# A fused attention and expert kernel: four buffers for the raw words of the dense weights, and their loads issued ahead

## Chip, core and metric

One Trainium2 chip, one core. The metric is the device time of one execution in microseconds (us); of several runs the median is given.

## What is computed

Three parts follow one another. Random-feature attention (4 batches, 8 heads, 576 positions, 64 wide, 128 features) makes `x` of 2304 rows by 512. A dense layer with a hidden width of 2048 follows, and then a layer of eight experts, of which each row takes one.

```python
q_p, k_p = phi(q_s), phi(k_s)              # exp(proj - sq - max), 128 features
num = q_p @ (k_p.T @ v); den = q_p @ k_p.sum() + 1e-6
x = num / den                              # 2304 x 512, heads side by side
h = x @ w_in                               # 512 x 2048, words of 64 bits
x = np.maximum(0.01 * h, h) @ w_out        # 2048 x 512, words of 64 bits
e = argmax(x @ w_gate)                     # one of 8 experts per row
out = gate * eom * (np.maximum(x @ w1[e], 0) @ w2[e])
```

`w_in` and `w_out` come in as float64, and so do not go into TensorE as they lie in memory: each has to be made into float32 on the core, and each float32 into a high part (`float32r`) and a low part. A product is three matmuls: high by high, high by low, low by high.

## The kernel before

**Tiles and loops.** The rows are cut into nine chunks of 256 (`c`), the hidden width into eight units of 256 (`u`). For each pair `(c, u)` `h_unit` makes the hidden values in PSUM (`hp`, 24 matmuls, L494 to L496) and evacuates them (`g`, L499 on ScalarE, then `gh` and `gl`), and `x_unit` multiplies by `w_out` into the accumulators (`acc`, 12 matmuls, L514 to L516). The pairs of the chunks 0 and 1 are woven (sorted by 2u, and 2u + 5 for chunk 1); then chunk follows chunk. In between, `tick` runs one stage of each attention item in flight: its loads (`xpair`, `nat`, `vb` on SyncE), squares (L284 on ScalarE), projection (`pw`, L313), exponentials (`h`, L342), transposes (`qtp`, `xtp`) and evacuations (`et`, `xh`, `xl`). `hp`, `qtp`, `xtp` and `nump` share two PSUM buffers at that time.

**The dense weights.** A unit has two half tiles of `w_in` and two of `w_out`; `order` lists the 32 half tiles, here called k = 0 to 31, unit by unit, `in` before `out`. `load_w` treats one:

- SyncE loads 512 KB of 64-bit words into `wraw` (L188 or L200). The tag has two buffers. `issue_after(newest[-1])` keeps the load behind the newest load of attention.
- ScalarE scales the upper words into `w` (L205; tag `w32`, two buffers).
- VectorE masks and shifts (L206), adds the sign (L207) and the lower word's bits (L208).
- ScalarE casts to the high part `wih` or `woh` (L210), GpSimd subtracts in two pieces to the low part `wil` or `wol` (L212).

The converted tiles lie in the ring `wring`, 32 places of 4 KB per partition; later the experts' weights go round in it. Before the pairs begin, k = 0 to 7 are treated. Then, in each step of chunk 0, `load_w` is called until 4(u + 2) half tiles are done, so the weights of unit u + 1 are treated in step u, just before the `h_unit` that reads them is written for the first of them.

**What sets the order.** The code is written in this sequence, and a scheduler orders each engine's instructions by when it expects them to be ready. Every engine then runs its queue in order and waits at the instruction whose inputs or buffer are missing. SyncE's queue holds all loads but the gathers.

Of the kernel before, what the change touches and what calls it, by code (L numbers as in the profile page):

```python
# [14 lines left out]
I32 = mybir.dt.int32  # L15
# [6 lines left out]
P = 128  # L22
# [21 lines left out]
WPRE = 8  # L44
WFROM = 0
WU = 6
TAIL = 9
# [40 lines left out]
def tile_kernel(ctx: ExitStack, tc: tile.TileContext, kT, k_nat, v_nat, qT, q_nat, om, w_in, w_out, wg, w1, w2, out, stop=None, dbg=None):  # L88
    nc = tc.nc
# [3 lines left out]
    wring = ctx.enter_context(tc.tile_pool(name="wring", bufs=32))  # L93
# [39 lines left out]
    wst = ctx.enter_context(tc.tile_pool(name="wst", bufs=2))  # L133

    with ExitStack() as pa:
# [41 lines left out]

        def load_w(kind, u, half, pool):

            raw = pool.tile([P, 512, 2], I32, name="wraw", tag="wraw")  # L180
            if kind == "in":
# [4 lines left out]
                wh, wl = win[u]  # L186
                with tc.issue_after(newest[-1]):
                    nc.sync.dma_start(raw.rearrange("p (i a) b -> p i (a b)", i=2),  # L188
                                      w_in[2 * half * P:2 * (half + 1) * P, u * 256:(u + 1) * 256].bitcast(I32).rearrange("(i p) a -> p i a", i=2))
                wh, wl = wh[:, 2 * half:2 * half + 2, :], wl[:, 2 * half:2 * half + 2, :]  # L190
                wh, wl = wh.rearrange("p a b -> p (a b)"), wl.rearrange("p a b -> p (a b)")
            else:
# [4 lines left out]
                wh, wl = wout[u]  # L197
                f = 2 * u + half
                with tc.issue_after(newest[-1]):
                    nc.sync.dma_start(raw.rearrange("p a b -> p (a b)"), w_out[f * P:(f + 1) * P, :].bitcast(I32))  # L200
                wh, wl = wh[:, half, :], wl[:, half, :]
            top, low = raw[:, :, 1], raw[:, :, 0]
            w = pool.tile([P, 512], I32, name="w32", tag="w32")

# [17 lines left out]
        order = [(k, u, h) for u in range(NU) for k in ("in", "out") for h in range(2)]  # L222
        loaded = 0
# [482 lines left out]
        for i in range(first + LEAD):  # L706
            tick(seq.pop(0) if i < first + NEW else None)
            while loaded < min(WPRE, (i - WFROM) * WPRE // (first + LEAD - WFROM)):
                load_w(*order[loaded], wst)
                loaded += 1  # L710
# [207 lines left out]
        for i, (c, u) in enumerate(pairs):  # L918
# [9 lines left out]
            while c == 0 and loaded < min(len(order), max(4 * (u + 2), WPRE + int(u * (32 - WPRE) / WU))):  # L928
                load_w(*order[loaded], wst)
                loaded += 1  # L930
            if i + 1 < len(pairs):
                gg[pairs[i + 1]] = h_unit(*pairs[i + 1])
# [191 lines left out]
```

## Time and profile before

| what | us |
|---|---|
| median of 3 runs (821.76 to 823.11) | 822.12 |
| the profiled execution | 822.98 |
| its span, first to last instruction | 821.3 |
| TensorE's matmuls busy in the span | 802.7 |
| VectorE busy | 440.0 |
| ScalarE busy | 370.0 |
| GpSimd busy | 161.0 |

The span is what lies between the first and the last instruction on the core; 1.7 us of the execution lie around it. The busy times are sums over stages that have different limits, so for this change the stretch from 46 us (the first `hp`) to 160 us (the last converted weight) is to be read by itself. Granted clock of TensorE: 1.00 of full speed (2.4 GHz) in each 20 us from the start to 200 us.

### The profile page before, as it was taken

What the parts mean: (1) busy time and instruction counts of PE and PEld (TensorE: products, weight loads), DVE (VectorE), ACT (ScalarE), POOL (GpSimd) and SP (SyncE); (2) the same over time, 40 slices, a digit from 0 to 9 for tenths busy, and PEclk for the clock granted to TensorE, in tenths of its full rate; (3) what the DMA queues carried; (4) which work ended last, traced back from release to release, by engine and by line L of the source; (5) the groups of instructions that cost most, each with busy time, mean ns of one, the idle gap of its engine ahead of it and who ended that gap; (6) DMA issues with size and microseconds to landing.
All of it is one profiled execution on the core that took longest, in us unless ns stands there. A gap on an engine that the chain in (4) does not pass through costs nothing. (4 is left out here: it accounts for less than half of the span.)

```text
span 821.3 us, 15800 instructions
## 1 busy us (share of the span) xinstructions
PE 802.7 (98%) x6061; PEld 712.0 (87%) x6061; DVE 440.0 (54%) x1118; ACT 370.0 (45%) x1239; POOL 161.0 (20%) x204
## 2 busy tenths in 40 slices
PE   9999999999999999999999999999999999999996
PEld 6777777888898988898899898888889989999995
DVE  6987799736645654544554543545644444343220
ACT  4886778625545656426435233122323343332210
POOL 3524444301211211011010000021014231130101
PEclk9999999999999999999999999999999999999998
DMA  6735665403312342022011000037316654150101
GB/s 211 229 124 178 176 194 181 141 1 91 66 47 61 94 67 59 26 44 70 28 33 21 27 1 1 27 114 99 78 34 205 171 166 140 58 163 24 46 14 34
DMA packets 45153, 72.74 MB, mean 89 GB/s; under 512 B 5905, under 2 KB 27665, under 8 KB 45074
## 3 DMA queue, kind: packets, MB, share of 16 engines
q1 hardware_dynamic: 41554, 62.22, 27.6%
q0 software_dynamic: 3520, 9.47, 3.8%
q8 instruction: 49, 0.80, 0.5%
q14 instruction: 30, 0.25, 0.1%
HBM read 61.08 MB, written 10.59 MB: 87 GB/s over the span
## 5 line engine op out<-in xcount | busy, mean ns | idle before, releaser
L494 PE MATMUL hp<-xh,wih 128*128 128x256 f32 x576 | 163.6, 284 | 0.8 <-ACT g L499 0.4
L496 PE MATMUL hp<-xh,wil 128*128 128x256 f32 x576 | 161.4, 280 | 2.0 <-POOL wil L212 2.0
L495 PE MATMUL hp<-xl,wih 128*128 128x256 f32 x576 | 161.1, 280 | 0.6 <-DVE xl L219 0.6
L514 PE MATMUL acc<-woh,gh 128*128 128x512 f32 x288 | 117.1, 406 | 1.2 <-ACT h L342 1.2
L516 PE MATMUL acc<-woh,gl 128*128 128x512 f32 x288 | 114.6, 398 | 0.1
L515 PE MATMUL acc<-wol,gh 128*128 128x512 f32 x288 | 114.7, 398 | 0.0
L494 PEld LDWEIGHTS hp<-xh,wih 128*128 128x128 f32 x576 | 108.1, 188 | 3.8 <-ACT g L499 0.5
L496 PEld LDWEIGHTS hp<-xh,wil 128*128 128x128 f32 x576 | 108.1, 188 | 3.5 <-POOL wil L212 3.2
L495 PEld LDWEIGHTS hp<-xl,wih 128*128 128x128 f32 x576 | 108.1, 188 | 2.7 <-DVE xl L219 1.0
L342 ACT ACTIVATE h<-pw,bias 128x128 f32<-128x128 f32 x288 | 84.2, 370 | 33.1 <-DVE bias L334 25.9
L501 DVE SCALAR_TENSOR_TENSOR g<-hp,g 128x512 f32<-128x512 f32 x56 | 38.6, 689 | 97.0 <-ACT g L499 96.6
L499 ACT COPY g<-hp 128x512 f32<-128x512 f32 x72 | 42.2, 587 | 100.6 <-PE hp L496 96.7
L795 PE MATMUL eht<-exh,ewh 128*128 128x256 f32 (+1 forms) x256 | 76.6, 299 | 0.0
L797 PE MATMUL eht<-exh,ewl 128*128 128x256 f32 (+1 forms) x256 | 75.5, 295 | 0.0
L796 PE MATMUL eht<-exl,ewh 128*128 128x256 f32 (+1 forms) x256 | 75.5, 295 | 0.0
L219 POOL TENSOR_TENSOR rawl<-xpair,rawh 128x256 fp32r<-128x256 f32 x38 | 29.0, 763 | 204.6 <-ACT rawh L216 198.8
L284 ACT ACTIVATE nat<-nat 128x64 f32<-128x64 f32 x224 | 55.4, 257 | 27.8 <-DVE bias L334 19.3
L798 ACT ACTIVATE ehh<-eht 128x256 fp32r<-128x256 f32 (+1 forms) x64 | 26.4, 412 | 91.3 <-PE eht L797 89.9
L516 PEld LDWEIGHTS acc<-woh,gl 128*128 128x128 f32 x288 | 54.1, 188 | 13.0 <-DVE gl L219 1.0
L514 PEld LDWEIGHTS acc<-woh,gh 128*128 128x128 f32 x288 | 54.1, 188 | 11.7 <-ACT h L342 1.4
L515 PEld LDWEIGHTS acc<-wol,gh 128*128 128x128 f32 x288 | 54.1, 188 | 9.2
L799 DVE SCALAR_TENSOR_TENSOR ehl<-eht,ehh 128x256 fp32r<-128x256 f32 (+1 forms) x64 | 29.2, 456 | 52.8 <-ACT ehh L798 49.2
(176 smaller groups left out, 1668.3 us busy)
## 6 DMA issues: line engine op xcount, KB each, us to landing
eraw<-w SPq DMA_DIRECT2D x32, 512.0 KB
wraw<-w_in SPq DMA_DIRECT2D x16, 512.0 KB
wraw<-w_out SPq DMA_DIRECT2D x16, 512.0 KB
x_d<-rows SPq DMA_DIRECT2D x9, 514.0 KB
xpair<-qT SPq DMA_DIRECT2D x18, 256.0 KB
nat<-k_nat SPq DMA_DIRECT2D x27, 128.0 KB
xpair<-kT SPq DMA_DIRECT2D x12, 256.0 KB
nat<-q_nat SPq DMA_DIRECT2D x23, 128.0 KB
```

The costliest lines, as they stand in the source:

```text
L284: nc.scalar.activation(nat[:, j], nat[:, j], AF.Square, scale=math.sqrt(sc * sc / 2.0), accum_out=s2[:, j:j + 1])
L342: st["e_last"] = nc.scalar.activation(h[:, j, :], src[:, j // 2, j % 2], AF.Exp, bias=bias[:, j:j + 1], scale=sc).ins
L494: nc.tensor.matmul(hp[:, i, :], a, xh[:, d, :], start=d == 0, stop=False)
L495: nc.tensor.matmul(hp[:, i, :], a, xl[:, d, :], start=False, stop=False)
L496: nc.tensor.matmul(hp[:, i, :], b_, xh[:, d, :], start=False, stop=d == ND - 1)
L499: last_g[:] = [nc.scalar.copy(g, hp).ins]
L514: nc.tensor.matmul(acc[t], a, h_, start=u == 0 and i == 0, stop=False)
L515: nc.tensor.matmul(acc[t], a, l_, start=False, stop=False)
L516: nc.tensor.matmul(acc[t], b_, h_, start=False, stop=u == NU - 1 and i == 1)
L795: nc.tensor.matmul(t, wh, self.xh[:, d, 0:n], start=d == 0, stop=False)
L796: nc.tensor.matmul(t, wh, self.xl[:, d, 0:n], start=False, stop=False)
L797: nc.tensor.matmul(t, wl, self.xh[:, d, 0:n], start=False, stop=d == ND - 1)
```

## The change

Two tiles `spare` are taken from the ring `wring` ahead of all others, as 64-bit raw buffers. The load is cut out of `load_w` into `fetch_w(k)`. For k = 8 to 27 the two halves of `w_out` (k % 4 is 2 or 3) go into the spare tiles, the halves of `w_in` into the two `wraw` buffers as before; k below 8 and from 28 on use `wraw` alone. After the conversions of a step of chunk 0 the loads of the next four half tiles are issued, so that they are in the queue one step earlier. The conversion itself, its `w` buffers and the amount of data are as they were. The ring has 32 places for 34 requests now: the last two (`w_out` of unit 7) take the places of the spare tiles.

```diff
--- before.py
+++ after.py
@@ -43,6 +43,7 @@
 LAG = 2
 WPRE = 8
 WFROM = 0
+SPARE = 2
 WU = 6
 TAIL = 9
 KQ = 8
@@ -175,18 +176,37 @@
         win = [None] * NU
         wout = [None] * NU
 
-        def load_w(kind, u, half, pool):
-
-            raw = pool.tile([P, 512, 2], I32, name="wraw", tag="wraw")
+        spare = [wring.tile([P, 512, 2], I32, name="wspare", tag="w") for _ in range(SPARE)]
+        raws = {}
+
+        def fetch_w(k):
+
+            kind, u, half = order[k]
+            if WPRE <= k < 28 and k % 4 >= 2:
+                raw = spare[k % 4 - 2]
+            else:
+                raw = wst.tile([P, 512, 2], I32, name="wraw", tag="wraw")
+            raws[k] = raw
+            with tc.issue_after(newest[-1]):
+                if kind == "in":
+                    nc.sync.dma_start(raw.rearrange("p (i a) b -> p i (a b)", i=2),
+                                      w_in[2 * half * P:2 * (half + 1) * P, u * 256:(u + 1) * 256].bitcast(I32).rearrange("(i p) a -> p i a", i=2))
+                else:
+                    f = 2 * u + half
+                    nc.sync.dma_start(raw.rearrange("p a b -> p (a b)"), w_out[f * P:(f + 1) * P, :].bitcast(I32))
+
+        def load_w(k):
+
+            if k not in raws:
+                fetch_w(k)
+            raw = raws[k]
+            kind, u, half = order[k]
             if kind == "in":
                 if win[u] is None:
                     wh = wring.tile([P, ND, 2 * P], F32R, name="wih", tag="w")
                     wl = wring.tile([P, ND, 2 * P], F32R, name="wil", tag="w")
                     win[u] = (wh, wl)
                 wh, wl = win[u]
-                with tc.issue_after(newest[-1]):
-                    nc.sync.dma_start(raw.rearrange("p (i a) b -> p i (a b)", i=2),
-                                      w_in[2 * half * P:2 * (half + 1) * P, u * 256:(u + 1) * 256].bitcast(I32).rearrange("(i p) a -> p i a", i=2))
                 wh, wl = wh[:, 2 * half:2 * half + 2, :], wl[:, 2 * half:2 * half + 2, :]
                 wh, wl = wh.rearrange("p a b -> p (a b)"), wl.rearrange("p a b -> p (a b)")
             else:
@@ -195,12 +215,9 @@
                     wl = wring.tile([P, 2, D], F32R, name="wol", tag="w")
                     wout[u] = (wh, wl)
                 wh, wl = wout[u]
-                f = 2 * u + half
-                with tc.issue_after(newest[-1]):
-                    nc.sync.dma_start(raw.rearrange("p a b -> p (a b)"), w_out[f * P:(f + 1) * P, :].bitcast(I32))
                 wh, wl = wh[:, half, :], wl[:, half, :]
             top, low = raw[:, :, 1], raw[:, :, 0]
-            w = pool.tile([P, 512], I32, name="w32", tag="w32")
+            w = wst.tile([P, 512], I32, name="w32", tag="w32")
 
             nc.scalar.activation(w.bitcast(F32), top.bitcast(F32), AF.Copy, scale=2.0 ** -112)
             nc.vector.tensor_scalar(w, w, 0x0FFFFFFF, 3, op0=ALU.bitwise_and, op1=ALU.logical_shift_left)
@@ -706,7 +723,7 @@
         for i in range(first + LEAD):
             tick(seq.pop(0) if i < first + NEW else None)
             while loaded < min(WPRE, (i - WFROM) * WPRE // (first + LEAD - WFROM)):
-                load_w(*order[loaded], wst)
+                load_w(loaded)
                 loaded += 1
 
 
@@ -926,8 +943,12 @@
                 at = [(ps_x, "x"), (ps_x, "x")] if c != 1 else [(ps_proj, "pj"), (ps_a, "a")]
                 acc[c] = [ps.tile([P, D], F32, name=f"acc{t}", tag=tag) for t, (ps, tag) in enumerate(at)]
             while c == 0 and loaded < min(len(order), max(4 * (u + 2), WPRE + int(u * (32 - WPRE) / WU))):
-                load_w(*order[loaded], wst)
+                load_w(loaded)
                 loaded += 1
+            if c == 0:
+                for k in range(loaded, min(len(order), loaded + 2 + SPARE)):
+                    if k not in raws:
+                        fetch_w(k)
             if i + 1 < len(pairs):
                 gg[pairs[i + 1]] = h_unit(*pairs[i + 1])
             if c == NCH - 1 and u == 0:
```

The lines shift: what was L188 is L192, L200 is L196, L205 is L222, L210 is L227, L216 is L233, L253 is L270, L267 is L284, L342 is L359, L401 is L418, L433 is L450 and L499 is L516.

SyncE's queue from the load of k = 7 (the first row) on; `wraw` and `wspare` are raw words, `xpair`, `nat` and `vb` attention's. Before:

```order
L200 DMA wraw<-w_out 128x1024
L253 DMA xpair<-kT 128x2x256 x2
L267 DMA nat<-k_nat 128x256 x2
L188 DMA wraw<-w_in 128x2x512 x2
L267 DMA nat<-k_nat 128x256
L200 DMA wraw<-w_out 128x1024
```

And changed:

```order
L196 DMA wraw<-w_out 128x1024
L270 DMA xpair<-kT 128x2x256
L192 DMA wraw<-w_in 128x2x512
L196 DMA wspare<-w_out 128x1024 x2
L192 DMA wraw<-w_in 128x2x512
L284 DMA nat<-k_nat 128x256
L270 DMA xpair<-kT 128x2x256
L284 DMA nat<-k_nat 128x256
L192 DMA wraw<-w_in 128x2x512
```

The loads of k = 8, 10, 11 and 9 stand ahead of one `xpair` and the first `nat`; before, k = 8 and 9 stood behind these and behind a second `nat`.

ScalarE's queue about the copy `g` of the eighth hidden unit in order of pairs (`g_1713`); `w32_1648`, `w32_1658`, `w32_1670` and `w32_1680` are the words of k = 20 to 23 in the kernel before:

```order
L210 CAST wih_1645<-w32_1648 128x512
L205 ACTIVATE w32_1658<-wraw_1656 128x512
L499 COPY g_1713<-hp_1688 128x512
L401 COPY kv1_1258<-kvp_1544 128x132
L216 CAST gh_1716<-g_1713 128x512
L205 ACTIVATE w32_1670<-wraw_1666 128x512
L210 CAST wih_1645<-w32_1658 128x512
L433 COPY et_1768<-qtp_1763 128x512
L210 CAST woh_1667<-w32_1670 128x512
L205 ACTIVATE w32_1680<-wraw_1678 128x512
```

Changed, at the same `g`; `w32_1674` is k = 23, and `w32_1917`, `w32_1925`, `w32_1935` and `w32_1943` are k = 24 to 27:

```order
L222 ACTIVATE w32_1917<-wraw_1682 128x512
L227 CAST woh_1664<-w32_1674 128x512
L222 ACTIVATE w32_1925<-wraw_1684 128x512
L516 COPY g_1713<-hp_1688 128x512
L227 CAST wih_1915<-w32_1917 128x512
L418 COPY kv1_1262<-kvp_1546 128x132
L233 CAST gh_1716<-g_1713 128x512
L222 ACTIVATE w32_1935<-wspare_141 128x512
L227 CAST wih_1915<-w32_1925 128x512
L222 ACTIVATE w32_1943<-wspare_142 128x512
L450 COPY et_1768<-qtp_1763 128x512
```

At the same place the queue is four half tiles further on, and L222 (L205 before) of k = 25 and 27 stands directly behind the cast of k = 23 and 25, whose word lay in the buffer that it writes.

## Rows read from the trace of the kernel before

**Rows 1.** Table by stretches: us, busy us (count) of PE, PEld, DVE, ACT, POOL.

```profile
70.00:122.00 52.00, 49.31 (x389) 40.44 (x389) 43.36 (x81) 36.77 (x128) 19.54 (x23) 1.00 0.59 180
122.00:160.00 38.00, 36.41 (x276) 29.12 (x275) 34.89 (x79) 29.57 (x109) 17.62 (x22) 1.00 0.55 175
46.00:160.00 114.00, 107.26 (x844) 87.44 (x845) 96.99 (x206) 87.20 (x323) 46.14 (x54) 1.00 0.56 172
...
200.00:300.00 100.00, 100.00 (x862) 89.33 (x858) 55.02 (x162) 52.94 (x235) 17.37 (x21) 1.00 0.30 65
```

**Rows 2.** Waits of TensorE, 46 to 160 us: total us, times, longest.

```profile
PE hp L496 <- POOL wil L212: 2.0, 5, 0.6
PE acc L514 <- ACT h L342: 1.2, 1, 1.2
PE pw L313 <- ACT h L342: 1.0, 2, 0.7
PE hp L495 <- DVE xl L219: 0.6, 1, 0.6
PE qtp L431 <- ACT g L499: 0.5, 1, 0.5
PE qtp L431 <- DVE xr L451: 0.5, 1, 0.5
PE hp L494 <- ACT g L499: 0.4, 1, 0.4
```

**Rows 3.** Waits of TensorE's weight loads, 46 to 160 us.

```profile
PEld hp L496 <- POOL wil L212: 3.2, 6, 0.8
```

**Rows 4.** Timeline of SyncE: start us, us, line, transfer.

```profile
53.86 0.34 SPq L267 DMA_DIRECT2D nat<-k_nat  x1
54.30 0.89 SPq L188 DMA_DIRECT2D wraw<-w_in  x2
...
74.44 0.38 SPq L188 DMA_DIRECT2D wraw<-w_in  x1
```

**Rows 5.** Timeline of ScalarE about half tile k = 13; idle time before in brackets.

```profile
78.33 0.67 ACT L205 ACTIVATE w<-wraw 128x512 f32<-128x512 f32 x1 [2.70 <-DMA wraw<-w_in]
...
79.89 1.13 ACT L342 ACTIVATE h<-pw,bias 128x128 f32<-128x128 f32 x4
...
82.54 0.62 ACT L210 CAST wih<-w 128x512 fp32r<-128x512 f32 x1 [0.53 <-DVE w L208]
83.06 0.66 ACT L205 ACTIVATE w<-wraw 128x512 f32<-128x512 f32 x1
```

**Rows 6.** Timeline of GpSimd: the subtractions of k = 9, 11 and 13.

```profile
65.90 2.33 POOL L212 TENSOR_TENSOR wil<-w,wih 128x256 fp32r<-128x256 f32 x2 [2.30 <-ACT wih L210]
...
74.45 1.44 POOL L212 TENSOR_TENSOR wol<-w,woh 128x256 fp32r<-128x256 f32 x2 [4.63 <-ACT woh L210]
...
83.24 1.61 POOL L212 TENSOR_TENSOR wil<-w,wih 128x256 fp32r<-128x256 f32 x2 [1.28 <-ACT wih L210]
```

**Rows 7.** Timeline of TensorE at the first of the waits for k = 13.

```profile
84.02 0.38 PE L496 MATMUL hp<-xh,wil 128*128 128x256 f32 x1 [0.31 <-POOL wil L212]
```

**Rows 8.** Waits of SyncE's queue, whole span.

```profile
SPq L200 <- DVE w L208: 43.4, 13, 11.0
```

**Rows 9.** Waits of ScalarE, 46 to 160 us.

```profile
ACT woh L210 <- DVE w L208: 6.5, 9, 1.5
...
ACT w L205 <- DMA wraw<-w_in: 3.2, 3, 2.7
...
ACT w L205 <- DMA wraw<-w_out: 0.9, 3, 0.4
```

**Rows 10.** Lines by themselves: count, ns min/median/max, first and last start us.

```profile
L206 DVE TENSOR_SCALAR w<-w x32: 397/418/1023, 15.4 to 154.2; 128x512 int32<-128x512 int32 x32
...
L207 DVE SCALAR_TENSOR_TENSOR w<-wraw,w x32: 670/693/1240, 16.2 to 154.8; 128x512 int32<-128x512 int32 x32
...
L208 DVE SCALAR_TENSOR_TENSOR w<-wraw,w x32: 674/691/1233, 17.9 to 155.9; 128x512 int32<-128x512 int32 x32
...
L212 POOL TENSOR_TENSOR wol<-w,woh x28: 731/750/1197, 46.7 to 158.1; 128x256 fp32r<-128x256 f32 x28
```

## The prediction

> **What bounds the kernel now.** TensorE does. I first read the table by stretches [rows 1]: from 200 to 300 us it is busy for all of 100.00 us, so later than that nothing that another engine does shows in the time. In the stretch where the dense weights are converted beside attention, 46 to 160 us, it is busy for 107.26 of 114.00 us. The 6.74 us that are missing there are all that this change can win directly, and they stay won, because TensorE has no slack behind them. The table of TensorE's waits in that stretch [rows 2] says what they are: 2.0 us in five waits for the low half of `w_in`, which GpSimd makes (L212); the next lines are a wait of 1.2 us and two waits of 1.0 us for `h` of ScalarE, and 0.5, 0.5 and 0.4 us for other buffers. A weight load that waits costs a little more than the idle time of the matmul unit: the load is normally hidden behind the matmul before it, and its own waits for L212 come to 3.2 us [rows 3]. So late weights cost between 2.0 and 3.2 us; the rest belongs to ScalarE and VectorE, which are busy for 87.20 and 96.99 of the 114 us [rows 1].
>
> Then I asked why the weights are late. One half tile (k = 13, the second of hidden unit 3) shows the chain: its load is issued at 74.44 us [rows 4], ScalarE sits idle for 2.70 us until it lands and starts L205 at 78.33 [rows 5], VectorE makes the word, ScalarE casts at 82.54, GpSimd subtracts from 83.24 to 84.85 [rows 6], and TensorE has waited for the first half of that at 84.02 [rows 7] and waits for the second. The load was late because a raw buffer comes free only when the half tile two before it is through VectorE; SyncE stood for 43.4 us in 13 waits of that kind [rows 8]. The half tiles k = 8 and 9 have the same fault: issued at 54.30 behind attention's loads [rows 4], and the second one subtracted only from 65.90 on [rows 6], where TensorE waits again.
>
> **The change, part by part.**
>
> Four raw buffers and early loads. No instruction and no byte is added: 32 loads, 32 conversions, the same matmuls. In the order on SyncE the load of k = 8 stands ahead of two attention loads that it stood behind, with both spare loads at its side. The second of those two alone went out at 53.86 [rows 4], so the load goes some us earlier than 54.30. From there on a load waits for the half tile four before it. ScalarE's waits for raw words, 3.2 + 0.9 us in six waits [rows 9], should go. A wait for the word from VectorE (L210, 6.5 us for `woh` alone [rows 9]) shrinks too, since more stands between the two instructions in the new order.
>
> What that gives on TensorE. In the new order on ScalarE the cast of k = 9 and that of k = 13 stand further ahead of the copy `g` of the unit that reads them; counting the instructions that stand between with ScalarE's pace (four `h` in 1.13 us, 0.52 us from a cast to the next start [rows 5]), the lead grows from about 3.2 to 5.1 us for k = 9 and from 4.4 to 6.9 us for k = 13, and for units 4 to 7 from 4 to 9 us up to 11 to 20 us. The longest of the five waits is 0.6 us [rows 2]. All five go: 2.0 to 3.2 us; I take 2.6.
>
> What moves. The conversions get done sooner: by the copy `g` of the ninth unit 28 are through VectorE, not 24. Between the third and the ninth of these copies (70 to 122 us) VectorE gets 16 conversions for 13. One costs it 0.42 + 0.69 + 0.69 = 1.80 us [rows 10], so 5.4 us more on 43.36 of 52 us [rows 1]: 94% busy. From 122 to 160 us four fall away, 7.2 us of 34.89. In that later stretch, at 92% today, TensorE loses 38.00 - 36.41 = 1.59 us [rows 1]; I take half of that as won, 0.8 us, with 0 and 1.6 as ends. So a VectorE at 92 to 94% goes with a loss of TensorE of about 4%, no more than the 2.69 of 52 us that it loses in the earlier stretch now.
>
> What is added: a wait of ScalarE for GpSimd. The converted word has two buffers as before, and L205 of k overwrites the word of k - 2, which GpSimd reads until its second subtraction ends. The trace of before has no such wait, because the raw words came later than that. A pair of subtractions takes 1.44 to 2.33 us [rows 6] after the cast. In the new order L205 stands with less than 1.4 us of ScalarE's work behind the cast of k - 2 in 13 places, where it did in 4; for k = 25 and 27 it stands directly behind. Over the 13 the work between comes to 8.4 us, so ScalarE would stand for 13 x 1.44 - 8.4 = 10.3 us at least, against 4.1 us for raw words that it stands for now. Behind a standing L205 are queued `g`, `et` and the exponentials `h` on ScalarE; for them wait TensorE's next users of the two `h` PSUM buffers and of `pw`. ScalarE stands idle for 114.00 - 87.20 = 26.8 us of the stretch already, and TensorE's waits that ScalarE caused (1.2, 1.0 in two, 0.5, 0.4 [rows 2]) come to 3.1 us in five: one such wait is 0.6 us. I take two more of them, 1.2 us; the ends are none and eight (4.8 us), from the thirteen places less those where a wait for TensorE or for VectorE stands behind anyway.
>
> Attention's loads on SyncE: one of `xpair` and one of `nat` now stand behind four loads of 512 KB. The first load that shows it by itself took from 74.44 to about 78.3 us [rows 4, 5]. None of TensorE's waits that [rows 2] lists is for an attention load (two left out there are 0.2 us each), so I take nothing; the price, if that cover is gone, is one ScalarE wait like the 2.70 us of [rows 5], and a fourth of it (26.8 us of ScalarE's idle time go with 6.74 us of TensorE's) on TensorE, 0.7 us.
>
> The places of the converted weights: the two spare tiles are taken first of the ring, so the last pair (`wout` of unit 7) gets them back after k = 27 is converted, far ahead of k = 30, and the ring's order behind that is unchanged. Nothing.
>
> The sum: -2.6 - 0.8 + 1.2 = -2.2 us. The profiled execution took 822.98 us, its span 821.3: 819.1 of span, 820.8 in all. That execution was 0.86 us over the median of the three runs, so I forecast 822.12 - 2.2 = 819.9 us.
>
> **The rivals.**
>
> 1. The new waits give it back. With five waits of 0.6 us in place of two, the sum is -2.6 - 0.8 + 3.0 = -0.4: 821.7 us. For it: thirteen places by count. Against: ScalarE stands already for 26.8 us of the stretch, and much of the new standing takes the place of its waits for VectorE and for raw words.
>
> 2. Slower: VectorE and GpSimd get in each other's way. The trace shows two durations for one instruction: L207 takes 0.69 us in the middle and 1.24 at most, L212 0.73 at least and 1.20 at most [rows 10]. With conversions close behind one another, the subtraction of one lies beside L207 and L208 of the next. The Trainium skill ("SBUF — State Buffer", Who interferes with whom) says that a DVE instruction with two SBUF inputs contends with a GpSimd instruction that reads SBUF, and that one of them blocks for the whole of the other; the two durations here agree with that, while how often they meet in the new order no trace shows yet. If each of the 13 places has the long pair (2.33 us), ScalarE stands for 13 x 2.33 - 8.4 = 21.9 us, and all eight waits come: 4.8 us, with the gain at its low end, 2.0, and nothing from the later stretch: +2.8, 824.9 us. It decides from about seven such waits on. For it: VectorE at 94% in that stretch. Against: today's 92% from 122 to 160 us goes with little loss.
>
> 3. The loads don't come sooner, because SyncE is held by attention's loads that wait for their buffers (as 53.86 before 54.30 in the old order). Then L205 still waits for words and the time is 822.1 us. Against: the new order puts the loads ahead of those.
>
> **How the numbers follow.** A measurement of this kernel can tell about 0.2%, 1.64 us, from no change: faster is under 820.48, slower over 823.76. The forecast gets 0.50, with its own range 817.4 (all of 3.2 and 1.6, no new wait) to 820.5; the first rival 0.30, the third 0.05, both within 0.2%; the second 0.15. Faster 0.50, same 0.35, slower 0.15. The range leaves out about 0.05 below 817.4 and 0.10 of the slower case above 824.2.
>
> **What would show it.** Right: no wait of TensorE for L212 between 46 and 160 us; no wait of ScalarE for raw words after k = 9; waits of L205 for L212 on ScalarE of 10 us or more, a line that the trace of before doesn't have; VectorE busier before 122 us and less busy behind it; TensorE's busy time over 109 of the 114 us. Wrong: waits of TensorE for `h`, `g` or `et` of ScalarE that together exceed 4 us (rival 1, and 2 with long L207 and L212), or L205 still waiting for raw words (rival 3). The order of the later stages is the same, so a difference that arises after 200 us would be outside all of this.

## The result, and the profile after

The changed kernel takes 831.3 us (median of 6 runs), against 822.05 us for the kernel before on the same chip: ratio 1.0115, 95% interval 1.0098 to 1.0132. It is slower by 9 us, where the prediction said 2 us faster, and lies outside its range. The profiled execution took 830.27 us with a span of 828.5 (before: 822.98 and 821.3).

First the table by stretches of the changed kernel: us; busy us (count) of PE, PEld, DVE, ACT, POOL; TensorE's granted clock; DMA share; GB/s. It answers to [rows 1].

```profile
0.00:830.00 830.00, 806.23 (x6061) 715.11 (x6061) 441.71 (x1118) 369.60 (x1239) 160.84 (x204) 0.99 0.31 88
70.00:122.00 52.00, 44.60 (x340) 36.64 (x340) 43.51 (x75) 38.24 (x135) 23.64 (x26) 0.93 0.63 194
122.00:160.00 38.00, 35.95 (x244) 28.46 (x245) 30.48 (x74) 25.57 (x91) 14.35 (x18) 0.96 0.37 119
46.00:160.00 114.00, 103.63 (x776) 83.48 (x776) 94.86 (x195) 82.83 (x304) 47.00 (x54) 0.96 0.55 171
200.00:300.00 100.00, 100.00 (x857) 89.60 (x855) 57.23 (x182) 54.34 (x243) 16.63 (x20) 1.00 0.28 71
```

Nothing is lost after 200 us. Between 46 and 160 us TensorE is idle for 10.37 us, before for 6.74. And its granted clock, 1.00 there before, averages 0.96, so that its busy time grows too. Over the whole span, 806.23 us busy and 22.3 idle stand against 802.67 and 18.6 before: of the 7.2 us of span, half (3.6 us) is slow matmuls and half idle time.

The waits of TensorE in that stretch (total us, times, longest) answer to [rows 2], those of ScalarE to [rows 9]:

```profile
PE pw L330 <- ACT kv L418: 2.4, 1, 2.4
PE acc L531 <- ACT kv L418: 2.2, 1, 2.2
PE nump L461 <- ACT et L450: 2.1, 1, 2.1
PE kvp L399 <- ACT kv L418: 0.9, 1, 0.9
```

```profile
ACT w L222 <- POOL wol L229: 7.9, 6, 2.4
ACT w L222 <- POOL wil L229: 6.4, 6, 1.8
...
ACT woh L227 <- DVE w L225: 3.2, 5, 1.2
...
ACT w L222 <- DMA wraw<-w_in: 1.6, 1, 1.6
```

The wait for late weights is gone from the first list, which was the aim; the copies `kv` and `et` of ScalarE stand in its place. The second list has the wait that the kernel before did not have: the scaling L222 (L205 before) stands for GpSimd's subtraction L229 (L212 before), 14.3 us in twelve waits. How the one makes the other is read from ScalarE's timeline (start, us, and in brackets the idle time before):

```profile
87.96 0.62 ACT L227 CAST woh<-w 128x512 fp32r<-128x512 f32 x1
...
90.62 0.66 ACT L222 ACTIVATE w<-wraw 128x512 f32<-128x512 f32 x1 [1.79 <-POOL wol L229]
91.18 0.60 ACT L227 CAST wih<-w 128x512 fp32r<-128x512 f32 x1
91.69 0.37 ACT L359 ACTIVATE h<-pw,bias 128x128 f32<-128x128 f32 x1
91.95 0.58 ACT L516 COPY g<-hp 128x512 f32<-128x512 f32 x1
92.42 0.28 ACT L418 COPY kv<-kvp 128x132 f32<-128x132 f32 x1
```

```profile
88.66 1.93 POOL L229 TENSOR_TENSOR wol<-w,woh 128x256 fp32r<-128x256 f32 x2 [3.04 <-ACT woh L227]
```

```profile
92.75 0.50 PE L531 MATMUL acc<-woh,gh 128*128 128x512 f32 x1 [2.25 <-ACT kv L418]
```

GpSimd reads the word until 90.6; L222 wants that word's buffer; the `kv` copy stands in the same queue four instructions behind it; TensorE stands for 2.25 us. It is so too at 121.18 us (L222 waits for 2.41 us, then `kv`, TensorE 2.39) and at 69.92, where L222 waits for only 1.04 us, then `et`, and TensorE stands for 2.11. The other nine waits of L222, 9.1 us together, have no stop of TensorE of over 0.9 us behind them.

The price doesn't end there. The same table in steps of 2 us about the stop at 72 us:

```profile
70.00:72.00 2.00, 0.00 (x0) 0.00 (x0) 1.35 (x3) 2.00 (x5) 0.84 (x1) 1.00 0.94 301
72.00:74.00 2.00, 1.89 (x28) 1.68 (x29) 2.00 (x3) 1.66 (x7) 1.50 (x2) 0.71 0.07 27
74.00:76.00 2.00, 2.00 (x10) 1.02 (x8) 1.85 (x6) 1.00 (x9) 0.00 (x0) 0.50 0.34 60
76.00:78.00 2.00, 2.00 (x20) 1.76 (x20) 1.11 (x5) 1.66 (x6) 1.11 (x2) 0.94 0.96 330
```

Behind the stop the granted clock falls to 0.50, the 1.2 GHz level: ten matmuls in 2 us. After the stops that end at 92.75 and 123.05 us it falls again. Three such falls, in steps of 20 us a clock of 0.91 each, go with the 3.6 us of slow matmuls. The split is that of one execution: a second profile of the same kernel (830.6 us, the run "after again" below) has one fall, 2.5 us more of busy time than before and 5.1 us more of idle time.

### The profile page after: what moved, and what is told of

Its sections match the earlier page's. It is cut to its first block, busy times and chain, and to the rows that moved or that the text cites. A ratio compares the mean times of both kernels' runs of the same rounds, so it can differ in the third digit from the quotient of the medians.

```text
span 828.5 us, 15794 instructions
## 1 busy us (share of the span) xinstructions
PE 806.2 (97%) x6061; PEld 715.1 (86%) x6061; DVE 441.7 (53%) x1118; ACT 369.6 (45%) x1239; POOL 160.8 (19%) x204
## 5 line engine op out<-in xcount | busy, mean ns | idle before, releaser
L532 PE MATMUL acc<-wol,gh 128*128 128x512 f32 x288 | 116.4, 404 | 0.0
L359 ACT ACTIVATE h<-pw,bias 128x128 f32<-128x128 f32 x288 | 84.2, 368 | 34.2 <-DVE bias L351 32.2
L516 ACT COPY g<-hp 128x512 f32<-128x512 f32 x72 | 42.2, 587 | 103.8 <-PE hp L513 103.6
L301 ACT ACTIVATE nat<-nat 128x64 f32<-128x64 f32 x224 | 55.6, 260 | 28.2 <-DVE bias L351 19.1
```

Source lines behind the costliest of these rows:

```text
L301: nc.scalar.activation(nat[:, j], nat[:, j], AF.Square, scale=math.sqrt(sc * sc / 2.0), accum_out=s2[:, j:j + 1])
L359: st["e_last"] = nc.scalar.activation(h[:, j, :], src[:, j // 2, j % 2], AF.Exp, bias=bias[:, j:j + 1], scale=sc).ins
L516: last_g[:] = [nc.scalar.copy(g, hp).ins]
L532: nc.tensor.matmul(acc[t], a, l_, start=False, stop=False)
```

## The experiments

The theory that these rows suggest (A): ScalarE, which takes its instructions in order, stands at L222 for the word buffer that GpSimd holds, and what is queued behind it comes late to TensorE. The rivals: the early loads disturb the queues; the new buffers or their places cost by themselves; conversions that run ahead cost through VectorE and ScalarE whoever holds a buffer (D); GpSimd beside VectorE slows both (rival 2 of the prediction). Ratios are to the kernel before on the same chip, with 95% intervals.

### Four raw buffers without early loads; early loads without them

The loop of early fetches was taken out of after:

```
-            if c == 0:
-                for k in range(loaded, min(len(order), loaded + 2 + SPARE)):
-                    if k not in raws:
-                        fetch_w(k)
```

> The changed kernel without the loop that issues loads ahead: four raw buffers, each load issued where its half tile is treated. The conversions are spread about as in the kernel before (the 20th is done before the ninth copy g, not before the seventh), but in ScalarE's queue 11 scalings stand with less than 1.44 us of work behind the cast two before. Theory A: ScalarE waits for GpSimd for 8 us or more, at least one TensorE wait over 1.5 us, 825 to 831 us. Theory B: not crowded, so 821 to 823 us. Theory C: no early loads, so 821 to 823 us.

830.6 us, 1.0117 (1.0102 to 1.0132), as slow as after. TensorE's waits for late low parts are back (2.1 us in five), and ScalarE stands for GpSimd for longer still:

```profile
ACT w L222 <- POOL wil L229: 11.4, 8, 2.4
...
ACT w L222 <- POOL wol L229: 4.6, 3, 2.5
```

Then the reverse, two raw buffers with the loop kept:

```
-SPARE = 2
+SPARE = 0
-            if WPRE <= k < 28 and k % 4 >= 2:
+            if SPARE and WPRE <= k < 28 and k % 4 >= 2:
```

> The changed kernel without the spare tiles: two raw buffers as before, and loads issued two ahead. In ScalarE's queue 2 scalings stand with less than 1.44 us of work behind the cast two before (before: 4, changed: 13). Theory A: ScalarE waits for GpSimd for under 3 us, no wait of TensorE over 1.4 us, clock 1.00, and the waits of TensorE for the low half of w_in (2.0 us before) gone: 819 to 822 us. Theory B: conversions a little earlier than before, 820 to 823 us. Theory C: early loads ahead of attention's, 824 us or more.

825.5 us, 1.0039 (1.0026 to 1.0053). So the early loads are not what costs most; the buffers are, by the order that they allow. But a small loss, which A did not expect, remains.

### The wait at L222 taken away: by order, and by more word buffers

In one version L222 is held back behind the cast of the half tile before; it then never stands for GpSimd:

```
+            with ExitStack() as held:
+                if k > WPRE:
+                    held.enter_context(tc.issue_after(casts[-1]))
+                nc.scalar.activation(w.bitcast(F32), top.bitcast(F32), AF.Copy, scale=2.0 ** -112)
```

> The changed kernel with one edge more: from the tenth half tile on, the scaling on ScalarE (L222) is queued behind the cast (L227) of the half tile just before it. Four raw buffers and early loads stay. In ScalarE's queue no scaling then stands with less than 1.44 us of work behind the cast of the half tile two before; in the changed kernel 13 do. Theory A (ScalarE stands at the scaling for the word buffer that GpSimd still reads, the copies kv and et behind it come late, TensorE waits over 2 us three times and its clock falls each time): ScalarE's waits for GpSimd fall from 14.3 us to under 3, no wait of TensorE over 1.4 us, granted clock 1.00 from 46 to 160 us, 819 to 822 us. Theory B (the conversions are done too densely for VectorE and GpSimd): this order spreads them as before did, so 820 to 823 as well; it does not tell A from B. Theory C (the early loads hold attention's loads back on SyncE): the loads are as early as in the changed kernel, so over 827 us with the same three waits.

827.1 us, 1.0073 (1.0048 to 1.0098), over a wide spread of runs (823.1 to 830.9; the profile is of the fastest). In another, one of the two spare tiles holds two more word buffers:

```
-SPARE = 2
+SPARE = 1
+        words = wring.tile([P, 2, 512], I32, name="words", tag="w")
+            if WPRE <= k < 28 and k % 4 >= 2:
+                w = words[:, k % 4 - 2, :]
```

> The changed kernel with the two places of the ring shared out otherwise: one is a third raw buffer, the other is cut into two more word buffers, so there are three raw and four word buffers; loads go three ahead. The conversions are done as early as in the changed kernel (16 or 20 of them by the same copies g), but the scaling overwrites the word of the half tile four before. Theory A: no wait of ScalarE for GpSimd to speak of (under 3 us), no TensorE wait over 1.4 us, clock 1.00, 819 to 823 us. Theory B: VectorE is as crowded as in the changed kernel, so 826 us or more, with waits of TensorE for VectorE's or ScalarE's results. Theory C: 826 us or more.

824.1 us, 1.0029 (1.0017 to 1.0040): 7 us better than after. Both directions are as A says, both sizes are short of it. To see whether the buffers as such cost, the kernel before got the two more word buffers alone; its order stays as it is:

> The kernel before with two more buffers for the converted words (four in all) out of the ring of converted weights; raw words keep their two buffers, no load is issued earlier, and the order of the instructions on every engine is that of the kernel before. In the kernel before ScalarE shows no wait for GpSimd's hold on these buffers in any row of its waits between 46 and 160 us. Theory A (after is slow because ScalarE stands for word buffers in its new order, and TensorE's stops then halve its clock) expects no change: 821 to 823 us, no stretch of 20 us before 200 us with a granted clock under 0.97. Theory B (more buffers and a changed placement of the tiles in SBUF cost by themselves, which would explain that the versions without these waits are still 2 to 5 us over before) expects 824 to 826.

821.9 us, 1.0004 (0.9991 to 1.0017). Places and buffers by themselves cost nothing that can be told from no change.

### What a late ScalarE copy costs

In the kernel before, a copy of n x 128 elements was put ahead of three of the `kv` copies:

```
+                if (b, p) in ((1, 0), (1, 1), (0, 1)):
+                    nc.scalar.copy(pause, kvs[b, p][:, None, 0:128].to_broadcast([P, n, 128]))
                 nc.scalar.copy(kvt[b][:, 2 * p:2 * p + 2, :], kvs.pop((b, p))[:, 0:2 * HV])
```

> The kernel before with one ScalarE copy of 128x768 elements from PSUM ahead of three of the four kv copies (about 74, 101 and 115 us); by the cast of 128x512 that takes 0.51 us each pause is 0.75 us, and nothing else is changed, though the scheduler may shift other instructions. It measures what TensorE loses when ScalarE's kv copy comes later. Theory A says that stops of TensorE of about a microsecond cost only themselves: 0.75 us or less at each of three places, no fall of the granted clock, 822 to 824.5 us. Rival (any shift of ScalarE's order costs as much as after's): 828 or more.

825.8 us, 1.0054 (1.0037 to 1.0071): 4.4 us for three pauses of 0.80 us, more than A allowed.

> As the run with 768 elements, but each of the three pauses is a copy of 128x2048, 1.9 us by the same cast, close to ScalarE's longest stops for GpSimd in after (1.8 and 2.4 us). Theory A expects three TensorE waits for the kv copy of 1.5 to 2.2 us, each followed by some 3.5 us at a granted clock near 0.5, so that each place costs 1.5 to 2.2 us of wait and some 1.8 us of slow matmuls: 821.6 + 3 x 3.7 = 832 us, 827 to 834. If the clock's fall has another cause than TensorE's stop, the three waits alone stand: 825 to 828. If the kv copies have slack that covers 1.9 us: 822 to 824.

830.1 us, 1.0110 (1.0079 to 1.0141): 8.8 us for three pauses of 1.87 us. The total is what A expected, the way there is not. The three pauses start at 28, 75 and 89 us (in the run with 768 elements at 28, 76 and 86), not at about 74, 101 and 115, so the first of them lies ahead of the stretch. The profile shows one wait of TensorE for `kv`, of 1.4 us, and a stretch at low clock that comes much later.

```profile
PE acc L517 <- ACT kv L404: 1.4, 1, 1.4
```

```profile
148.00:152.00 4.00, 4.00 (x23) 4.00 (x22) 2.86 (x10) 2.87 (x10) 1.51 (x3) 0.57 0.48 164
```

Time taken from ScalarE comes back as 1.6 to 1.8 times as much in the total, but not at the place. Of the 7.8 us by which the span grew in the second run, 3.6 are slower matmuls, and 2.7 are lost by TensorE before 46 us. The added copies also shift the order on ScalarE and VectorE, so these two runs do not give the price of a late `kv` copy.

### The hold moved to another buffer

The last step writes the finished word into the raw buffer, so that GpSimd holds one of four raw buffers instead of one of two word buffers:

```
-            nc.vector.scalar_tensor_tensor(w, low, 29, w, op0=ALU.logical_shift_right, op1=ALU.bitwise_or)
-            wf = w.bitcast(F32)
+            nc.vector.scalar_tensor_tensor(top, low, 29, w, op0=ALU.logical_shift_right, op1=ALU.bitwise_or)
+            wf = top.bitcast(F32)
```

> The changed kernel, but the last step of the conversion writes the finished word into the upper half of the raw words' buffer and the cast and GpSimd's subtraction read it there, so the word buffer (still two) is given back by VectorE's or-ing at L225 rather than by GpSimd's subtraction at L229, one cast and one subtraction (0.5 to 1.2 us) earlier; the raw words' buffers (four) are held longer instead. Theory A expects ScalarE's waits for a word buffer to shrink from 14.3 us to some 3 to 7 us, none over 1.5 us, TensorE's waits for kv and et copies under 1.5 us, and 823 to 827 us. If the dense conversions themselves (VectorE and GpSimd at work close together) were what costs, it stays at 829 to 831.

828.9 us, 1.0097 (1.0070 to 1.0123): a miss. No wait for GpSimd is left, but ScalarE now stands at the next link of the chain, the cast, and at the exponentials' `bias`, both VectorE's; its waits and TensorE's:

```profile
ACT h L359 <- DVE bias L351: 8.2, 8, 1.6
...
ACT woh L227 <- DVE wspare L225: 4.0, 4, 2.3
```

```profile
PE pw L330 <- ACT h L359: 2.8, 2, 1.8
PE nump L461 <- ACT g L516: 2.3, 2, 1.2
PE pw L330 <- ACT kv L418: 2.0, 1, 2.0
```

The conversions come in bursts there, with GpSimd at work beside them. From 100 to 120 us:

```profile
100.00:120.00 20.00, 16.18 (x129) 13.34 (x128) 18.98 (x31) 14.17 (x48) 11.42 (x14) 1.00 0.71 220
```

VectorE is busy for 18.98 of 20 us with 31 instructions, and TensorE loses 3.82 of them. With this run, A alone did not hold.

### Sooner without any new buffer

In the kernel before, each half tile is loaded and converted one place sooner:

```
-            while c == 0 and loaded < min(len(order), max(4 * (u + 2), WPRE + int(u * (32 - WPRE) / WU))):
+            while c == 0 and loaded < min(len(order), max(4 * (u + 2) + 1, WPRE + int(u * (32 - WPRE) / WU))):
```

> The kernel before with no buffer added, but each half tile of weights loaded and converted one place sooner in the program (four times the unit plus nine rather than plus eight). It does by itself what the change wants, low parts that are there in time, with raw words still setting the pace. By ScalarE's order one half tile instead of four has under 1.44 us of work ahead of its scaling. TensorE's five waits of 2.0 us for low parts go. Theory A expects a gain of that size or nothing: 819.5 to 822. If an earlier conversion by itself costs (VectorE and ScalarE late for the attention's own steps), 824 to 827.

828.9 us, 1.0069 (1.0042 to 1.0097). Again A is wrong: with two raw buffers, and one wait for GpSimd (1.6 us), the kernel loses some 6 us. In its profile, which is of the slowest of the four runs (834.4 us), ScalarE stands for raw words (7.6 us in eight waits) and TensorE for `h`, `gh` and `kv`:

```profile
PE pw L313 <- ACT h L342: 2.8, 4, 1.3
PE acc L514 <- ACT gh L216: 2.1, 1, 2.1
PE acc L514 <- ACT kv L401: 1.4, 1, 1.4
PE acc L514 <- ACT h L342: 1.3, 1, 1.3
```

What these losses share is that conversions are asked for sooner; what GpSimd has to do with it was asked next.

### GpSimd taken out of the conversion

From the ninth half tile on GpSimd's subtraction was left out, in before and in after; the low parts are one tile of zeros `wz`, TensorE's work is unchanged:

```
+                    wl = wring.tile([P, ND, 2 * P], F32R, name="wil", tag="w") if u < 2 else wz
-            for a in range(0, 512, 256):
+            for a in range(0, 512 if k < WPRE else 0, 256):
```

> The kernel before with GpSimd's subtraction left out from the ninth half tile on: the low parts of those weights are one tile of zeros, so the work of TensorE is the same and the dense layers' low parts are missing from the result. ScalarE's order is that of the kernel before. It is the base for the next run. TensorE's five waits of 2.0 us in all for the low parts go, and with them 24 x 2 subtractions on GpSimd beside which VectorE's instructions took up to 1.24 us instead of 0.69. Expected 818.5 to 821 us by all theories.

817.0 us, 0.9926 (0.9899 to 0.9954), less than was expected. TensorE is idle for 1.54 us of the stretch, where the kernel before loses 6.74:

```profile
46.00:160.00 114.00, 112.46 (x891) 94.46 (x890) 86.23 (x207) 88.29 (x323) 3.89 (x6) 1.00 0.57 172
```

> The changed kernel with the same left out (low parts of the dense weights are zeros from the ninth half tile on): nothing of GpSimd holds a word buffer, and nothing of it runs beside VectorE's conversions; ScalarE still scales and casts early and close together (13 half tiles with under 1.44 us of work of its own between the cast two before and the scaling, as in after). Theory A, that GpSimd's part (its hold on the word buffers) makes after slow, expects it within 2 us of the run of the kernel before without low parts: 818.5 to 822.5. Theory D, that the conversions come in bursts in ScalarE's and VectorE's order and the steps wait for one another whoever holds the buffer (as the run with the word written back showed at the cast), expects 824 or more, with TensorE's waits for h, kv and et copies of 1.5 us and over.

819.1 us (median of nine of the ten runs; the tenth took 828.1), 0.9962 (0.9941 to 0.9983): some 12 us under after, and TensorE is hardly idle in this stretch:

```profile
46.00:160.00 114.00, 112.99 (x892) 95.65 (x891) 85.15 (x209) 88.89 (x326) 4.99 (x6) 1.00 0.54 172
100.00:120.00 20.00, 20.00 (x154) 16.60 (x153) 18.81 (x45) 18.50 (x62) 0.00 (x0) 1.00 0.77 247
```

Conversions that run ahead, about as close behind one another as in after (13 places), cost TensorE nothing in this stretch: it is idle for 1.01 us, against 1.54 in the version of before. (The totals are 2 us apart, within their intervals.) From 100 to 120 us VectorE is about as full as in the run with the word written back (18.81 and 18.98 us), but with 45 instructions in place of 31, and TensorE is not idle at all. So D as it stands falls: GpSimd's part is needed for the loss. In the next version of after GpSimd works but holds no word (it subtracts the cast weights from themselves; low parts zero):

```
-                nc.gpsimd.tensor_sub(wl[:, a:a + 256], wf[:, a:a + 256], f32(wh[:, a:a + 256]))
+                nc.gpsimd.tensor_sub(wl[:, a:a + 256], (f32(wh) if k >= WPRE else wf)[:, a:a + 256], f32(wh[:, a:a + 256]))
```

> The changed kernel with GpSimd's subtraction reading the cast weights twice instead of the word buffer (the low parts come out as zeros from the ninth half tile on): GpSimd works as long as in after and beside VectorE as in after, but holds no word buffer. ScalarE's order is that of the run without low parts. Theory A (the hold alone) expects that run plus up to 1.5 us for TensorE's waits for late low parts. Rival 2 of the prediction (GpSimd beside VectorE) expects at least 3 us more than that run, with VectorE's conversion instructions near 1.2 us in the bursts.

818.6 us, 0.9955 (0.9938 to 0.9972).

```profile
46.00:160.00 114.00, 108.69 (x856) 90.01 (x855) 92.67 (x205) 87.49 (x323) 42.63 (x54) 1.00 0.55 172
```

TensorE's idle time in the stretch is 5.3 us, half of after's. By the total it looked as if the hold were all. Two things speak against that. With one source instead of two GpSimd's pieces (128x256) also got shorter, 836 and 772 ns in the mean against 942 and 859 in after. And beside the run without low parts the stretch shows a loss that the totals hide: ScalarE's and VectorE's instructions stand in the same order in both (but for about ten records each), no word is held in either, and with GpSimd at work VectorE is busy for 92.67 us, not 85.15, and TensorE idle for 5.31, not 1.01. The total of the run without low parts contains a hole near 288 us (last section). So GpSimd beside VectorE costs TensorE some 4 us there, by one profile of each. Next the hold was removed with the computation kept.

### Four raw and four word buffers, and after again

```
+        words = wring.tile([P, 2, 512], I32, name="words", tag="w")
+            if WPRE <= k < 28 and k % 4 >= 2:
+                w = words[:, k % 4 - 2, :]
```

> The changed kernel with four buffers for the converted words as well as for the raw ones (two more out of the ring of converted weights); nothing is left out of the computation. The scheduler then puts ScalarE's scalings still further ahead, up to three half tiles ahead of a cast. If GpSimd's hold on two word buffers is the whole cause (theory A, as the run with the subtraction's other source says, 818.6 us against 831.3), it comes out near that run: 817 to 821 us, no ScalarE wait for GpSimd. If conversions that run ahead cost by themselves through ScalarE's and VectorE's order (theory D, as the run with one half tile sooner says, 828.9 us): 825 to 830, with TensorE's waits for h, kv, gh over 1.3 us.

826.9 us, 1.0057 (1.0040 to 1.0073). With L222 held behind the cast of the half tile two before, so that ScalarE's order is near that of the run with 818.6 us:

```
+                if k > WPRE:
+                    held.enter_context(tc.issue_after(casts[-2]))
```

> As the run with four raw and four word buffers, but from the tenth half tile on ScalarE scales a half tile only behind its cast of the one two before, so that its order is nearly that of the run with the subtraction's other source (a scaling straight behind the cast two before, in 16 of 24 places) without the hold of GpSimd that makes such a place stand in after. Theory A: 817 to 821 us. Theory D: 824 or more.

825.5 us, 1.0049 (1.0036 to 1.0062). On the same chip:

> The changed kernel once more, on the same chip as the two runs with four word buffers, for a comparison side by side: 829 to 833 us, TensorE waits of over 2 us for ScalarE's copies.

829.4 us, 1.0089 (1.0072 to 1.0105). Neither of the two versions shows a wait of ScalarE for GpSimd in its rows, and both lie where D expected them. So taking the hold away, with the order that goes with it, is worth 2.5 to 4 us of after's 8 here. What is left shows in the rows of the held version: ScalarE's largest wait, and two stretches of the table.

```profile
ACT h L367 <- DVE bias L359: 7.7, 8, 2.3
```

```profile
46.00:160.00 114.00, 105.28 (x819) 86.40 (x820) 97.37 (x202) 85.47 (x309) 50.36 (x54) 0.99 0.54 171
100.00:120.00 20.00, 15.87 (x112) 12.76 (x113) 19.80 (x34) 15.49 (x51) 12.85 (x14) 0.97 0.74 228
```

VectorE is full from 100 to 120 us (19.80 of 20). In 46 to 160 us it is busy for 97.37 us; in the version without GpSimd, with as many conversions, for 85.15. One instruction shows it best, the small `bias` that `h` waits for (count, busy us, mean ns), in the held version and without GpSimd's part:

```profile
L359 DVE TENSOR_TENSOR bias<-ngm,s 128x4 f32<-128x4 f32 x14 | 5.9, 420 | 0.1
```

```profile
L355 DVE TENSOR_TENSOR bias<-ngm,s 128x4 f32<-128x4 f32 x15 | 2.3, 155 | 0.2
```

155 ns become 420 in the mean (449 in after again, 322 in the version with the other source). But the waits of `h` go up to 2.3 us, and `bias` never takes more than 0.71: what is late is VectorE's queue ahead of it. The Trainium skill ("SBUF — State Buffer", Who interferes with whom) has VectorE instructions with two SBUF inputs contend with GpSimd for an exclusive lock; the rows agree. The kernel before has that neighbour too: there `bias` takes 261 ns in the mean, and VectorE is busy for 96.99 us [rows 1], no less than after's 94.86. The slowing by itself is therefore not new with the change; the close conversions and the hold are.

### The subtraction on VectorE

If GpSimd as a neighbour is the rest, moving its subtraction to VectorE should help although it adds VectorE work:

```
+            if k >= WPRE:
+                nc.vector.tensor_sub(wl, wf, f32(wh))
+            else:
                 for a in range(0, 512, 256):
```

> The changed kernel with the same move of the subtraction to VectorE. The word buffers are held by VectorE for 0.7 us rather than by GpSimd for 2, so ScalarE's 14.3 us of waits for GpSimd go, and VectorE's instructions are no longer slowed, but it has 16.6 us more of them. Theory (hold plus VectorE slowed beside GpSimd): under after by 4 to 9 us, 822 to 827. If VectorE's total load decides: 829 and more.

822.4 us, 1.0010 (0.9983 to 1.0037): 7 us under after (829.4), level with the kernel before, and nothing is left out of the computation.

```profile
46.00:160.00 114.00, 108.94 (x845) 89.08 (x844) 96.70 (x229) 88.63 (x323) 5.35 (x6) 1.00 0.56 172
```

VectorE is busy for 96.70 us, subtractions (16.4 us) included, within the 94.97 (after again) to 97.37 us that it takes with GpSimd doing them. The same lines in the kernel before:

> The kernel before with the low parts of the dense weights subtracted by VectorE instead of GpSimd from the ninth half tile on, the whole 128x512 in one instruction; nothing is left out. Each costs VectorE some 0.69 us, 24 x 0.69 = 16.6 us; against that stands what VectorE loses beside GpSimd (97.5 us of 114 busy with it, 86.2 without). Between 46 and 160 us VectorE comes to about 86.2 + 16.6 = 103 us of 114. If VectorE's own load decides, slower than before: 824 to 830. If GpSimd's slowness (1.9 to 2.2 us for a half tile) and its slowing of VectorE in the bursts decide, as the runs without low parts say, faster: 818 to 822.

823.3 us, 1.0018 (1.0003 to 1.0033), no gain, and between the two ranges. With every second half tile moved in after (`k >= WPRE and k % 2` in the condition above):

> The changed kernel with every second half tile's subtraction on VectorE (8.3 us more there) and the others on GpSimd. It tells whether a mixture is better than either: by the theory between after and the run with all on VectorE, 823 to 829.

823.8 us, 1.0013 (0.9994 to 1.0033), with 12.1 us of waits for GpSimd at L222 left. So most of the standing can stay and most of the loss go: these waits do not set the loss by their sum. No version that computes everything beats the kernel before.

## Why the prediction was wrong

**Right.** TensorE's waits for L212 are gone; ScalarE's waits for raw words shrank from 4.1 us [rows 9] to 1.6; SyncE's wait of [rows 8] fell from 43.4 to 31.0 us; the waits of the scaling for GpSimd, which the trace of before did not have, are there in twelve places (thirteen were counted), 14.3 us against "10.3 us at least". VectorE is busier before 122 us (64.4 us from 46 us on, before 62.1) and less busy behind it. Attention's loads behind four others cost nothing that the rows show.

**The step that failed** is the price of those waits on TensorE: "one such wait is 0.6 us. I take two more of them, 1.2 us; the ends are none and eight (4.8 us)". The 0.6 us was the mean of waits that a merely busy ScalarE causes [rows 2]. What was measured is four waits of TensorE for `kv` and `et`, 7.6 us (2.4 + 2.2 + 2.1 + 0.9). Three of the twelve standings, 5.2 us together, came back as 6.75 us; the other nine cost little. The prediction named the queued instructions as `g`, `et` and `h`; it did not look which of them has no slack, and missed `kv` altogether, though the trace of before has a wait of TensorE for it, of 0.2 us. This step is not the whole. The versions in which GpSimd subtracts in full but L222 hardly stands for it still take 824.1 to 828.9 us, so what moves with the early conversions, which the sum put at -0.8, costs some 2 to 7 us as well.

**A term that was missing**: TensorE's clock. Three stops were followed by stretches at half clock; busy time grew by 3.6 us of the 7.2 us of span (2.5 us in the second profile).

**The gain.** The late weights are repaid as forecast: the waits of 2.0 us are gone. The 0.8 us from the later stretch did not come; from 122 to 160 us TensorE loses 2.05 us, not less than 1.59 [rows 1]. "TensorE's busy time over 109 of the 114 us" became 103.63. In the working, one conversion was priced at 1.80 us by medians; by the means in the stretch before (454, 828 and 781 ns) it is 2.06. Of the ends of the range, 822.12 - 3.2 - 1.6 is 817.3, not 817.4, and 824.2 is worked out nowhere.

**The argument against rival 1** was that the new standing takes the place of the old. It did in part: `woh` for VectorE and raw words together fell from 10.6 us [rows 9] to 4.8. But the sum of ScalarE's standing does not give the time: the version with the word written back stands at its scalings and casts for 10.0 us in all, before for 14.3 and after for 19.1, and yet takes 828.9 us.

**Rival 2** had the right sign, at 0.15, and 824.9 us; its place is where part of the rest was found. But its ground, "VectorE at 94%" from 70 to 122 us, did not come: VectorE was busy for 43.51 of the 52 us, 84%, and the conversions done sooner fell before 70 us (20.86 of 24 us, before 18.74). A VectorE share is a bad witness either way: it was in no run above 86% of the 114 us, and 20 us at 19 to 19.8 go with 3.8 and 4.1 us of TensorE's time where GpSimd works beside it, 18.81 without GpSimd with none.

**What is shown and what stays open.** Shown: taking GpSimd's subtraction out of after, or giving it to VectorE, takes away the loss (819.1 and 822.4 us), so early conversion itself costs little and GpSimd's part in it is the cause. Its two ways of acting, the hold on the word buffers and the slowing of VectorE, are not separated in size. The slowing costs some 4 us of TensorE's idle time between two versions with the same order, but the kernel before has it too. Taking the hold away, in another order, gave 2.5 to 7 us in the versions that compute everything (826.9 to 824.1 us); yet 12.1 us of it stay in the version of 823.8 us. And two versions without the hold, in a similar order, are 7 us apart (818.6 and 825.5): in the first GpSimd's pieces are shorter, VectorE is busy for 4.7 us less and the low parts are zeros, and no run tells which of these counts. Open too: how much of the 0.39% of the version with early loads alone is the changed order of the instructions, since nearly every edit shifts it.

## What to carry to other kernels

A chain of stages has a buffer at each stage; giving more to the first moves the wait to the next scarce one, here from SyncE, where only loads stood behind it, to ScalarE, where TensorE's inputs did. Before adding buffers, count them along the chain, find the in-order queue in which the next wait will stand, and price it by the instruction behind it that has no slack, at the length of the standing, not at a mean of today's waits. And before a helper engine is made to work closer beside another, look at what it takes from its neighbour already: here it is seen in the mean duration of the neighbour's smallest instructions (155 ns alone, 261 before, 420 to 449 with close conversions).

## What the runs showed of the hardware

A stop of TensorE of 2.1 to 2.4 us in an otherwise busy stretch can be followed by half the clock (0.71 and 0.50 in two steps of 2 us above), which adds about half to the price of the stops (3.6 us beside 6.75). It does not always: in the second profile of the same kernel, the stop at 72 us was as long (2.12 us) and the clock stayed at 1.00, while matmuls after it were less dense.

```profile
70.00:72.00 2.00, 0.07 (x2) 0.00 (x0) 1.28 (x3) 2.00 (x4) 0.77 (x1) 1.00 0.82 251
72.00:74.00 2.00, 1.82 (x30) 1.58 (x30) 2.00 (x2) 1.65 (x6) 1.57 (x2) 1.00 0.19 78
74.00:76.00 2.00, 1.31 (x13) 0.88 (x12) 1.93 (x7) 1.86 (x12) 0.15 (x1) 1.00 0.27 80
```

In that profile only the stop at 122.4 us (2.39 us) was followed by a fall (0.50 from 122 to 128 us). What decides is not settled here.

Both versions without low parts have, in their profiled runs, a hole of some 6 us near 288 us in which TensorE waited for nothing that the profile shows, and its clock from 280 to 300 us averages 0.83 and 0.74; these are the waits of the one made from after, between 200 and 300 us. Their other runs go down to 815.2 and 815.5 us, about that much under the profiled ones.

```profile
PE hp L516 <- issue: 3.6, 1, 3.6
PE hp L517 <- issue: 2.1, 1, 2.1
```
